# Sixteen small products of a blank tile ahead of TensorE's program

## The chip, the cores and the metric

The kernel runs on one core of a Trainium2 chip. A core has five engines that work side by side, each from its own list of instructions: TensorE (PE; its weight loads are listed apart, as PEld), VectorE (DVE), ScalarE (ACT), GpSimd (POOL) and SyncE (SP). They wait for each other and for transfers through semaphores. The metric is device time in microseconds. The kernel before takes 306.78 us, the median of three runs (306.5 to 307.46).

## The reference

Windowed attention with 8 batches of 8 heads over 576 positions, head size 64, and behind it a two-layer block on the 4608 tokens:

```python
scores = scale * np.matmul(q, k.transpose(0, 1, 3, 2))
rel = pos[:, None] - pos[None, :]
mask_plain = (rel >= 0) & (rel < window)                                  # window 32, heads 0-3
mask_dil = (rel >= 0) & (rel < window * dilation) & (rel % dilation == 0) # dilation 4, heads 4-7
scores = np.where(masks[None, :, :, :], scores, -1000000000.0)
attn = softmax(scores)                         # over the keys, 1e-9 added to the sum
x = matmul(attn, v)                            # then tokens by 512 features
h = x @ w_in                                   # 512 -> 2048
out = (h * (1.0 / (1.0 + np.exp(-h)))) @ w_out # 2048 -> 512
```

## The kernel before

Attention is cut into blocks of 32 queries by 64 keys. z = 0 names the four plain heads, z = 1 the four dilated ones, whose positions are sorted into four classes so that they become plain windows too. For each block TensorE makes the scores (L364, L374 and L390), DVE adds the mask, takes the maximum and normalises, ACT takes exponentials (L568; L557 for a whole tile), DVE turns the probabilities round (L606), and TensorE multiplies them with v (L637) into the transposed attention output, which copies put into xT (L670, L672, L707, L712). Layer one (L721, and L746 for batch 0) multiplies xT with w_in, ACT applies the SiLU into gT (L729, L754), layer two (L766, L790) multiplies gT with w_out, and the rows leave through SP (L776).

The order on each engine is the order of the program's text, since the scheduling is by hand: `plan_of(b)` says before which step of batch b's two layers which piece of attention for batches b+1 and b+2 is issued. Batch 0 has no layers to hide behind, so it has a prologue of its own (L896 to L935), and its attention is done in two parts of 256 and 320 positions, named `part`. The prologue runs: transposes of k and q for part 0 (L302 and L313, which read gT's space, where `load_part` has put the rows), scores (L390, L374), softmax, transposes for part 1, products with v, scores for part 1. Then comes layer one of batch 0: four feature tiles at a time for part 0 (products 256 columns wide), then two at a time for part 1 (320 wide). In `plan_of(0)`, `values0` and `finish0` for part 1 are placed at steps -8 and -6, that is among the layer-one products of part 0: their 64 and 44 products with v (L637) stand between 256-column products, and the two copies of L712 on DVE finish what the 320-column products read.

The loads are issued by POOL in the order of the text: k and q of batch 0 in two parts (L135), v of batch 0 (L174, L183), w_in in four pieces (L191), q and k of batch 1 (L112, L119), w_out in four pieces (L197), v of batch 1, and later batches from `plan_of`, q and k of them by L152.

Buffers come from pools. `cpool` (named const) holds single tiles for the whole run, among them the identity, the masks, both weights and gT; the pools opened after it (nat for loaded q and k, msp, stat, pp, ptp, xtp, o32) lie behind it in SBUF. Two pools are in PSUM: big, two buffers of two banks each, and ps, four buffers of one bank each, which transposes, scores and products with v use in turn.

TensorE's list holds 8799 instructions, nearly all of them pairs of a weight load and a product. The first of them are those of `transpose0(1, 1, 0, act)`, which wait for k's first part.

## Time and profile before

| | |
|---|---|
| median of three runs | 306.78 us (306.5 to 307.46) |
| the profiled execution | 307.47 us |
| its span, from first to last instruction | 305.7 us |
| TensorE products | busy 292.6 us, 96% of the span, 4393 of them |
| weight loads | busy 186.8 us, 4393 |
| DVE, ACT, POOL | busy 193.1, 203.8 and 120.0 us |
| software DMA queue q0 | 107840 packets, 20.38 MB |
| instruction queue q8 | 34 packets, 0.56 MB |
| mean granted TensorE clock | 0.998 |

A line of a list by time gives the start and the length in us, the engine, the line of the kernel, the operation with the tiles out<-in, the shapes and how many instructions are merged into the line; in square brackets stands the idle time of that engine just before, and what ended it. "issue" there means that the profile shows nothing that the engine waited for. The chain of waits is followed back from the last instruction: each piece is what the next one had to wait for.

### The profile page before, as it was taken

Reading aid. Unit: us, or ns where it says so; the run is one execution under the profiler, and the core shown is the slowest. Engines: PE = TensorE matmul, PEld = TensorE weight load, DVE = VectorE, ACT = ScalarE, POOL = GpSimd, SP = SyncE. Lnnn points to the kernel's source line nnn. Section 1 sums busy time; section 2 is a strip of 40 time slices with the busy share of each in tenths; the row PEclk is TensorE's granted clock in tenths of the full one; section 3 lists DMA queues with packets and bytes.
Section 4 is the critical chain, followed back from the end, with each engine's and each line's share of the span. In section 5 each row is a group of like instructions: output and inputs, shape, how many; then the busy total and the mean of one; then the engine's idle time right before and its main releaser. Section 6 shows DMA issues by size and latency. Waiting matters only on the chain.

```text
span 305.7 us, 10277 instructions
## 1 busy us (share of the span) xinstructions
PE 292.6 (96%) x4393; PEld 186.8 (61%) x4393; DVE 193.1 (63%) x353; ACT 203.8 (67%) x685; POOL 120.0 (39%) x182
## 2 busy tenths in 40 slices
PE   2998999999989999999999999999999999999995
PEld 1666754677445775477644775478644775477544
DVE  1895579448898868866893768955893762810012
ACT  3676597765997559975895559975795559546200
POOL 8745347979963295236906086240000000000000
PEclk9999999999999999999999999999999999999999
DMA  8999999999993899399959199390002100110021
GB/s 102 159 204 207 207 161 171 195 184 126 121 187 71 94 67 131 109 116 38 121 74 186 38 59 136 104 119 4 3 34 105 36 2 34 52 56 0 17 88 69
DMA packets 113213, 30.47 MB, mean 100 GB/s; under 512 B 95520, under 2 KB 108688, under 8 KB 113168
## 3 DMA queue, kind: packets, MB, share of 16 engines
q0 software_dynamic: 107840, 20.38, 80.8%
q1 hardware_dynamic: 5328, 9.44, 8.6%
q8 instruction: 34, 0.56, 0.8%
q14 instruction: 11, 0.09, 0.1%
HBM read 40.75 MB, written 9.44 MB: 164 GB/s over the span
## 4 chain that ended last, share of the span: by engine, by line
PE 78%; DMA 8%; DVE 5%; POOL 3%; ACT 3%; issue 2%; DVEq 0%; POOLq 0%
PE h L721 32%; PE o L790 31%; PE h L746 5%; PE x L637 4%; PE o L766 3%; DMA w_in<-in_moe_w_in_dram 3%; DMA n<-in_q_dram 2%; DMA gT<-in_q_dram 2%; ACT pe L568 2%; PE s L364 2%; POOL n L152 2%; DVE pn L590 1%; DMA vw<-in_v_dram 1%; POOL gT L135 1%; DVE ob L775 1%
## 5 line engine op out<-in xcount | busy, mean ns | idle before, releaser
L729 ACT ACTIVATE gT<-h 128x576 f16<-128x576 f32 x112 | 72.8, 650 | 61.5 <-PE h L721 61.3
L790 PE MATMUL o<-w_out,gT 128*128 128x512 f16 (+1 forms) x528 | 113.8, 373 | 0.0
L721 PE MATMUL h<-xT,w_in 128*128 128x288 f16 x896 | 113.4, 287 | 0.0
L721 PEld LDWEIGHTS <-w_in 128*128 128x128 f16 x896 | 86.5, 98 | 23.6 <-issue 0.2
L790 PEld LDWEIGHTS <-gT 128*128 128x128 f16 x528 | 50.6, 98 | 55.4
L568 ACT ACTIVATE pe<-ms,nm 128x64 f32<-128x64 f32 x238 | 78.9, 333 | 0.1
L775 DVE COPY ob<-o 128x512 f32<-128x512 f32 (+1 forms) x35 | 22.9, 664 | 51.8 <-PE o L790 50.6
L568 ACT ACTIVATION_READ_ACCUMULATOR pe<-ms,nm 128x1 f32 x238 | 44.5, 187 | 0.0
L152 POOL DMA_DIRECT2D n<-in_k_dram x44 | 31.9, 736 | 26.1 <-DVE kC L337 25.1
L408 DVE SCALAR_TENSOR_TENSOR ms<-s,mask 128x512 f32<-128x512 f32 x28 | 19.2, 686 | 29.1 <-PE s L364 19.9
L152 POOL DMA_DIRECT2D n<-in_q_dram x44 | 32.0, 744 | 2.5 <-DMA n<-in_q_dram 2.5
L174 POOL DMA_DIRECT2D vw<-in_v_dram x32 | 18.3, 578 | 35.3 <-PE x L637 33.0
L590 DVE TENSOR_TENSOR pn<-pe,r 128x640 f16<-128x640 f32 (+2 forms) x32 | 26.2, 818 | 1.1
L606 DVE STREAM_TRANSPOSE pt<-pn 128x640 f16<-128x640 f16 (+4 forms) x32 | 24.7, 772 | 1.1
L183 POOL DMA_DIRECT2D vw<-in_v_dram x32 | 21.2, 672 | 10.0 <-DMA w_out<-in_moe_w_out_dram 7.8
L488 DVE TENSOR_REDUCE nm<-ms 128x10 f32<-128x640 f32 (+1 forms) x28 | 22.0, 787 | 1.0
L746 PE MATMUL h<-xT,w_in 128*128 128x256 f16 (+1 forms) x128 | 19.2, 304 | 1.6 <-DVE band L244 0.9
L637 PEld LDWEIGHTS <-vw 32*64 32x64 f16 (+1 forms) x1264 | 13.0, 107 | 7.4 <-issue 7.1
L637 PE MATMUL x<-pt,vw 32*64 32x64 f16 (+2 forms) x1264 | 14.9, 193 | 1.7 <-DVE pt L606 1.7
L746 PEld LDWEIGHTS <-w_in 128*128 128x128 f16 x128 | 12.5, 104 | 6.3 <-issue 1.5
L766 PE MATMUL o<-w_out,gT 128*128 128x512 f16 x64 | 14.5, 380 | 0.0
L670 DVE CAST xT<-x 128x288 f16<-128x288 f32 x24 | 9.3, 449 | 7.7 <-PE x L637 7.7
(92 smaller groups left out, 204.6 us busy)
## 6 DMA issues: line engine op xcount, KB each, us to landing
out_dram<-ob SPq DMA_DIRECT2D x35, 256.0 KB, 3.4
n<-in_k_dram POOLq DMA_DIRECT2D x24, 108.0 KB, 4.2
n<-in_q_dram POOLq DMA_DIRECT2D x24, 108.0 KB, 4.9
vw<-in_v_dram POOLq DMA_DIRECT2D x31, 80.0 KB, 4.0
vw<-in_v_dram POOLq DMA_DIRECT2D x32, 72.0 KB, 3.9
w_in<-in_moe_w_in_dram POOLq DMA_DIRECT2D x4, 512.0 KB, 9.5
w_out<-in_moe_w_out_dram POOLq DMA_DIRECT2D x4, 512.0 KB, 11.4
n<-in_k_dram POOLq DMA_DIRECT2D x20, 72.0 KB, 4.0
```

The costliest lines, as they stand in the source:

```text
L152: nc.gpsimd.dma_start(out=qk[b, z, which][o : o + QB], in_=bass.AP((q, k)[which].tensor, (b * H + z * HH + half * HH // 2) * S * D + x * Q ...
L488: nc.vector.tensor_reduce(out=nm[:, 0:w], in_=ms[:, 0:w], axis=AX.X, op=ALU.max, negate=True)
L568: nc.scalar.activation(pe[:, t, :], src[t], AF.Exp, bias=a["nm", z, hi][:, t : t + 1], scale=k, accum_out=l[:, t : t + 1],)
L590: nc.vector.tensor_tensor(pn[:, 0:w], a["pe", z, hi][:, 0:w], r[:, 0:w, None].broadcast_to([P, w, KB]), ALU.mult)
L606: nc.vector.transpose(out, src)
L637: nc.tensor.matmul(x[h // 2][h % 2 * D : h % 2 * D + D, col : col + wd], vws[b % 2][r, NB + kb * DIL + c if z else kb], turned_cols(b, pt[ ...
L721: nc.tensor.matmul(h[:, half, 0:HS], w_in16[:, c, f * P : f * P + P], xT[c // 2][:, c % 2, half * HS : half * HS + HS], start=(c == cs[0]) ...
L729: nc.scalar.activation(gT[:, f, s0 : s0 + S].rearrange("p (a c) -> p a c", a=2), h[:, :, 0:HS], AF.Silu)
L746: nc.tensor.matmul(hs[i // m][:, i % m, 0 : c1 - c0], w_in16[:, c, (f + i) * P : (f + i + 1) * P], xT[c // 2][:, c % 2, c0:c1], start=(c = ...
L766: nc.tensor.matmul(o, gT[:, f, t * P : (t + 1) * P], w_out16[:, f, :], start=(f == 0), stop=(f == NFF - 1),)
L775: copy(ob, o)
L790: nc.tensor.matmul(o[:, 0, 0:m], gT[:, f, t * P : (t + 1) * P], w_out16[:, f, cols], start=(f == 0), stop=(f == NFF - 1),)
```

## The change

A tile `blank` of 32x32 half-precision zeros is added at the end of the constant pool, zeroed by DVE ahead of the memset of `band`. A tile `lead` is taken from ps, and sixteen products of `blank` with itself are written into its first 32 partitions and columns, ahead of the first transposes. Nothing reads `lead`. TensorE's list grows by 16 weight loads and 16 products to 8831 instructions, DVE's by one memset; the order of all other instructions on every engine is as it was. The first weight load of the sixteen waits for the memset on DVE, and the first product of the fourth transposed tile (L313 for q of part 0), which now gets the buffer that `lead` had, waits for the last of the sixteen.

```diff
     band = cpool.tile([P, KB], F32, name="band")
+    blank = cpool.tile([W, W], F16, name="blank")
+    nc.vector.memset(blank, 0.0)
     nc.vector.memset(band[0:W], 0.0)
     load_part(1, 0)
     load_part(0, 0)
...
+    lead = ps.tile([P, 512], F32, tag="ps", name="lead")
+    for _ in range(16):
+        nc.tensor.matmul(lead[0:W, 0:W], blank, blank, start=True, stop=True)
     transpose0(1, 1, 0, act)
     build_mask_b()
     transpose0(0, 1, 0, act)
```

## The prediction

> **What bounds the kernel now.** I read the page first, then the chain of waits, then TensorE's products and weight loads in order of time over the first 40 us, and at last the DMA queues and the busy time in chosen stretches.

> From the page: TensorE is the bound as a whole, and one DMA queue carries instructions.

> ```profile
> PE 292.6 (96%) x4393; PEld 186.8 (61%) x4393; DVE 193.1 (63%) x353; ACT 203.8 (67%) x685; POOL 120.0 (39%) x182
> PEclk9999999999999999999999999999999999999999
> q8 instruction: 34, 0.56, 0.8%
> ```

> The idle 4% lies mostly at the front, where the new work goes. The chain of waits between 12.9 and 33.5 us:

> ```profile
> 12.93 8.59 DMA w_in<-in_moe_w_in_dram
> 21.52 0.05 issue
> 21.56 1.92 PE h L746 x16
> ...
> 25.64 0.87 DVE xT L712 x2
> ...
> 27.13 0.47 issue
> 27.61 2.21 PE h L746 x15
> ...
> 33.52 0.01 issue
> 33.53 1.12 PE h L746 x7
> ```

> Until 21.5 us transfers decide; from 25.6 on TensorE does, with a gap before 27.6. In the lists by time, TensorE's products at the front and its weight loads around the gap:

> ```profile
> 5.64 0.60 PE L302 MATMUL t<-ident,gT 64*128 64x64 f16 x8 [5.64 <-DMA gT<-in_k_dram]
> ...
> 8.40 0.45 PE L390 MATMUL s<-kC,qC 64*32 64x64 f16 x32
> ...
> 17.88 3.48 PE L746 MATMUL h<-xT,w_in 128*128 128x256 f16 x16 [0.46 <-DMA w_in<-in_moe_w_in_dram]
> 21.56 1.92 PE L746 MATMUL h<-xT,w_in 128*128 128x256 f16 x16 [0.21 <-DMA w_in<-in_moe_w_in_dram]
> ```

> ```profile
> 25.03 0.43 PEld L637 LDWEIGHTS <-vw 32*64 32x64 f16 x44 [0.21 <-issue]
> 25.48 0.88 PEld L746 LDWEIGHTS <-w_in 128*128 128x128 f16 x9
> 27.60 1.88 PEld L746 LDWEIGHTS <-w_in 128*128 128x128 f16 x15 [1.24 <-issue]
> ```

> ```profile
> 27.59:33.52 5.93, 5.92 (x128) 4.05 (x128) 1.87 (x4) 3.88 (x7) 3.82 (x7) 1.00 1.22 206
> ```

> The reader is to see three things. (1) TensorE has no work before 5.64. (2) The idle 1.24 us before 27.60 has no tile behind it: "issue". The weight load that starts there waits for no semaphore; the last cast it could be tied to, the two of L712, ends at 26.51. (3) The last fence (busy time in a stretch: its columns are TensorE's products and weight loads, then DVE, ACT, POOL, the granted clock, DMA share and GB/s): from that stop to the next "issue" stop, at 33.53, TensorE ran 128 products and 128 weight loads, 256 instructions exactly.

> That number names the resource. 0.56 MB in 34 packets of q8 is 16.4 KB each, and 8799 TensorE instructions make some 34 portions of 256. Asked by stretches of 2 us, the DMA view has one q8 packet in each, and its row of GB/s jumps where it starts: 12.75, 19.15, 25.15, 31.20, 37.15, 43.25. At 3.0% of 16 engines over 2 us each lasts 0.96 us. So a portion is used 2.4 us after its fetch starts (25.17 to 27.60; 31.20 to 33.53), and the next fetch starts 3.6 us after the portion is begun (27.60 to 31.20, 33.53 to 37.17). In this stretch, with the DMA engines full of loads, TensorE can't get through 256 instructions in under 6.0 us, and twice it stops for them: from 26.51 (the end of the wanted cast) to 27.60, 1.09 us, and 0.18 us before 33.53.

> [...]

> **The change part by part.** The sum is made against the profiled execution: 307.47 us, span 305.70, 1.77 around it. It stands 0.69 above the median of 306.78, so I add the sum to the median.

> *The memset.* Nearest rows: 85 ns for 32 columns, 112 for 64 (L230, L204); their starts stand 0.07 to 0.12 apart. It goes ahead of the zeroing of band, which POOL needs at 3.27, 2.3 us later, and DVE then idles 1.77 us to 3.35. Zero. Uncovered: 0.1. It might stretch POOL's first DMA issue, which ran beside such memsets for 0.81 against 0.69 for the next: 0 to 0.07; I take 0.

> *The sixteen products.* None of this size is in the trace. Cheapest row: 32 products of 64x32 weights in 0.45 us, 14 ns each; dearest: the eight of L302 in 0.60 us, 75 each. So 0.2 to 1.2 us, nearer the first as the weights are small. They can start when the memset ends, about 1.0, and end by 2.2; TensorE then still waits for in_k until 5.64. Zero; uncovered, 0.2 to 1.2.

> *Buffers and addresses.* lead takes one of the four ps buffers, so the fourth transpose tile (L313 for q, at 7.82) waits for the last of the sixteen, done 5 us before; no other wait changes, and the later tiles keep their order. The pools after const move up 64 bytes. No row prices that: k and q loads of one shape land in 4.2 and 4.9 us, so an address is worth less than 0.7 on one landing, either way, and none of those landings is what the chain waits for at 40 us. Zero.

> *The 32 instructions themselves.* This is the step with a price. They run in idle time, but every 256-instruction portion now begins 32 instructions earlier in the old code. Two effects.

> First, the chain of fetches starts earlier. The portion start whose crossing let the fetch of 12.75 go lies among the L374 scores at 9.3; moved by 32 it lies among the L390 scores at 8.40. TensorE's queue takes instructions ahead of running them (at 49.3 a fetch starts 0.5 us after its crossing is executed, not 3.6), which puts the old crossing near 8.5 and the new near 8.2: 0.3 earlier. Bounds: 0, if transfers ahead of it fix the fetch's start, and 0.9, if nothing is taken ahead. I take 0.3, by the row at 49.3.

> Second, the stop moves. The portion usable at 27.60 is now usable at 27.30, but it begins 16 pairs earlier: 9 of L746 and the last 7 of the 44 L637 products. In the trace those 7 start at 25.31, and from there to where the 27.60 work could have begun is 1.26 us (7 products, their two casts on DVE to 26.51, 0.06 for the semaphore; 9 of L746 at 0.109 beside them). Before, these 1.26 us ran ahead of the stop, hidden by the fetch; now they come behind it: 27.30 + 1.26 = 28.56 against 27.60, +0.96. The next portion is there at 33.2, and TensorE reaches its start at 32.96 + 0.96 = 33.9: the 0.18 stop goes, +0.78. The one after (39.2) is reached at 40.2, unhindered; no stop is seen there now either.

> Behind that TensorE waits twice, 0.37 at 72.6 and 1.31 at 89.3, both for DVE work that began on TensorE's own products (at 66.97 and 79.99), so these move along. What runs beside what on DVE and POOL at 86.7, where a multiplication of 0.83 us takes 1.65, may shift and give or take 0.3. Sum: **+0.78 us, 306.78 + 0.78 = 307.6**; with the bounds of the first effect (1.08 with no earlier start, 0.18 with 0.9) and that 0.3, -0.1 to +1.4.

> **The rivals.**

> *Fetches don't decide, or it is swallowed.* For it: most of the 34 portions show no stop, and the gap at 27.6 ends near the SiLU of L754 (26.57 to 27.59), so that could be the cause; against it, the products there use the other big buffer, and 256 between two stops. 306.8.

> *A stop vanishes (the other side).* If the portion now beginning in the L637 products is there by 25.3, no stop is left: -1.09 - 0.18, 305.5. It decides from a fetch that starts before 23.0, 2.2 us sooner than now. Against: the first crossing gains 0.9 at most; for: lags of 0.5 (49.3) exist when the DMA engines are less loaded.

> *More starvation.* If the moved starts meet short products (the 36 transposes at 39.4, the 64 scores at 66.5) when a fetch is late, another stop of about 1 us adds up: 308.5. It decides where a fetch starts less than 2.4 us before need; the nearest, at 64.5 for 66.94, has just that.

> *The clock.* The sixteen products of L746 at 17.88 stand 0.213 apart, those at 21.56 0.109: the array runs at half rate until about 21, though the granted clock is 1.00. If the new work raised it early, those at 17.88 would end at 19.6 and wait for w_in until 21.5 all the same: 306.8. [...]

> **How the numbers follow.** The shifted stop: 0.62. Nothing, by either reason: 0.15. A stop vanishes: 0.11. More starvation: 0.12. What a measurement of this kernel can tell from no change is about 0.3%, 0.92 us: the shifted stop's +0.78, with its bounds, lies beyond that in 0.25 of the 0.62. So slower 0.25 + 0.12 = 0.37, same 0.37 + 0.15 = 0.52, faster 0.11. The range leaves out the vanished stop and the upper part of the starvation: 306.3 to 308.5; the likeliest case's own is 306.7 to 308.2.

> **What would show it.** Sixteen products at about 1 us, and the first L302 still at 5.64. A weight load of L637, 7 from the end of its 44, after an idle 1.5 to 2 us marked "issue" and starting near 27.3; nothing of the kind before the first 128x320 products, which start near 28.6; 128 and 128 from stop to stop, if there is a second; the q8 jumps 0.3 us sooner. The prediction is wrong if the stop sits where it sat, if the L637 products run through, or if TensorE is 0.8 late at 40 us and not at the end.

## The result and the profile after

| | before | changed |
|---|---|---|
| median of 12 runs, us | 306.86 (306.08 to 307.96) | 309.25 (306.97 to 310.98) |
| ratio, 95% interval | | 1.0058, 1.0034 to 1.0082 |
| profiled execution, us (span) | 307.47 (305.7) | 310.91 (309.1) |
| its mean granted clock | 0.998 | 0.994 |

The change makes the kernel slower, by more than 0.3%. The median lies 0.75 us above the top of the forecast range (308.5) and 1.65 us above the forecast (307.6). The changed kernel also scatters more: 4.0 us from lowest to highest, against 1.9. Four of its twelve executions have a mean clock of 0.994 and are the four of 310.08, 310.42, 310.91 and 310.98 us (the profiled one is among them); the other eight have 0.999 or more and a median of 308.2. Ratios here and below are not quotients of the two medians, and leave out executions 1.5% or more above the fastest of their kernel (one and two of the 35 of the kernel before in the later sets).

The page of the changed kernel: 16 products and 16 weight loads more, no other count that matters, and one slice in which the clock was not fully granted.

```profile
PE 295.6 (96%) x4409; PEld 188.6 (61%) x4409; DVE 194.0 (63%) x354; ACT 203.8 (66%) x685; POOL 119.5 (39%) x182
PEclk9999999999998999999999999999999999999999
q8 instruction: 34, 0.56, 0.8%
```

TensorE's products of the changed kernel by time (start, length of the group, line, tiles, shape, count; in brackets the idle time ahead and what ended it). Line numbers are 2 higher than in the kernel before, so L639 is the old L637, L748 the old L746; from the new products on they are 5 higher.

```profile
0.93 0.61 PE L900 MATMUL lead<-blank 32*32 32x32 f16 x16 [0.93 <-DVE blank L205]
5.66 0.60 PE L304 MATMUL t<-ident,gT 64*128 64x64 f16 x8 [4.13 <-DMA gT<-in_k_dram]
...
26.11 0.50 PE L639 MATMUL x<-pt,vw 32*64 32x32 f16 x37
27.58 0.24 PE L639 MATMUL x<-pt,vw 32*64 32x64 f16 x7 [0.98 <-issue]
27.75 3.40 PE L748 MATMUL h<-xT,w_in 128*128 128x256 f16 x24
...
89.08 0.41 PE L639 MATMUL x<-pt,vw 32*64 32x64 f16 x28
91.20 0.66 PE L639 MATMUL x<-pt,vw 32*64 32x64 f16 x48 [1.71 <-DVE pt L608]
91.79 6.91 PE L792 MATMUL o<-w_out,gT 128*128 128x512 f16 x24
```

Three places matter. The sixteen products run in 0.61 us, in the dead time ahead of the first transpose, which still starts at 5.66. At 27.58 stands the moved stop, 37 into the group of 44, as foretold. And at 91.20 a wait has grown, with something new behind it: the 24 products of L792 take 6.91 us, where the kernel before has

```profile
87.60 0.41 PE L637 MATMUL x<-pt,vw 32*64 32x64 f16 x28
89.32 0.61 PE L637 MATMUL x<-pt,vw 32*64 32x64 f16 x48 [1.31 <-DVE pt L606]
89.86 5.36 PE L790 MATMUL o<-w_out,gT 128*128 128x512 f16 x24
```

Setting each TensorE instruction of the changed trace against the same one before gives where the time went. The delay is +0.75 us at 7.3, as a load landed later in that execution, and +1.08 at 25.3, ahead of the stop: the trace's clock record begins, at full rate, at 23.30 us there and at 21.10 in the kernel before, and up to then the first products of layer one stand 0.21 apart, not 0.11. The stop takes this delay up, since it ends 2.46 us after its fetch starts (27.58 against 25.12), as in the kernel before (27.60 against 25.18, 2.42), and not with TensorE's work. Behind it the delay is +1.17 at 33.5, then +1.48 at 72.6 (0.3 came near 56), +1.88 behind the wait at 91.2, and then 0.21 more with every product of L792 until it is +3.49 at 95; from there it stays (+3.35 at the end). So the loss is 1.2 at the stop, 0.3 near 56, 0.4 in the longer wait, 1.6 behind it.

The weight loads of the changed kernel around the stop, in the same columns, have the row that the prediction asked for; 37 pairs of the 44 end one portion, and the other 7 begin the next.

```profile
26.11 0.39 PEld L639 LDWEIGHTS <-vw 32*64 32x64 f16 x37 [0.21 <-issue]
27.58 0.14 PEld L639 LDWEIGHTS <-vw 32*64 32x64 f16 x7 [1.09 <-issue]
```

Now the wait. VectorE of the changed kernel up to the pt (the probabilities turned round) that ends it:

```profile
87.65 1.50 DVE L589 TENSOR_SCALAR r<-l 128x10 f32<-128x10 f32 x1
89.19 0.22 DVE L590 RECIPROCAL r<-r 128x10 f32<-128x10 f32 x1
89.44 0.82 DVE L592 TENSOR_TENSOR pn<-pe,r 128x640 f16<-128x640 f32 x1
90.30 0.84 DVE L608 STREAM_TRANSPOSE pt<-pn 128x640 f16<-128x640 f16 x1
```

and GpSimd of the same kernel at that time: its transfers' issues, then a subtraction of the maximum for batch 3 (the old L543).

```profile
85.43 2.62 POOL L152 DMA_DIRECT2D n<-in_q_dram  x4
88.06 1.05 POOL L545 TENSOR_TENSOR ms<-ms,nm 128x512 f32<-128x512 f32 x1
```

The TENSOR_SCALAR on ten columns, 0.13 to 0.17 us where it runs alone, takes 1.50 and ends 0.04 after GpSimd's operation. It began 0.41 ahead of that operation, under the last of the four transfer issues (87.39 to 88.05), and by its own length would have been through under that issue. So it was held through the rest of an issue and then the whole operation. In the kernel before it was the TENSOR_TENSOR of 0.83 that took 1.65:

```profile
86.74 1.65 DVE L590 TENSOR_TENSOR pn<-pe,r 128x640 f16<-128x640 f32 x1
```

```profile
85.11 2.65 POOL L152 DMA_DIRECT2D n<-in_q_dram  x4
87.74 1.54 POOL L543 TENSOR_TENSOR ms<-ms,nm 128x512 f32<-128x512 f32 x1
```

It too began under an issue and by its own length would have ended at 87.57, ahead of GpSimd's operation, which itself took 1.54 there, against 1.05 in the changed kernel. Here VectorE's row ends 0.89 us ahead of GpSimd's (88.39 against 89.28), not 0.04 behind it, and both are lengthened. What the two engines hold each other up over is in no trace.

That GpSimd's issues of transfers hold VectorE by themselves is seen where its operation has been taken out (a run described below):

```profile
86.58 0.39 DVE L591 TENSOR_SCALAR r<-l 128x10 f32<-128x10 f32 x1
```

This row ends with an issue of GpSimd (86.31 to 86.97). In the fourteen traces of this document 27 TENSOR_SCALARs of this line behind 30 us, 0.31 to 0.56 us long, end within 0.01 us of the end of an issue. It hangs on the moment: all 27 that begin 0.25 to 0.35 us into an issue are held (over 0.30 us long), and three of the 102 that begin at another point of one. The 0.3 us near 56 are of this kind: a TENSOR_SCALAR from 54.95 to 55.46, 0.51 long (0.17 in the kernel before), ends with an issue, and the products behind its pt come that much later.

Last, busy time in two neighbouring stretches of 3.41 us (TensorE's products, weight loads, DVE, ACT, POOL, then granted clock, DMA share, GB/s), of the changed kernel

```profile
87.98:91.39 3.41, 1.70 (x58) 0.83 (x59) 3.31 (x5) 3.41 (x22) 1.12 (x2) 1.00 1.88 192
91.40:94.80 3.40, 3.40 (x55) 1.43 (x42) 3.30 (x9) 3.40 (x20) 0.00 (x0) 0.53 0.51 126
```

and of the kernel before

```profile
87.98:91.39 3.41, 2.10 (x60) 1.22 (x56) 3.36 (x8) 3.41 (x21) 1.30 (x1) 1.00 1.65 227
91.40:94.80 3.40, 3.40 (x17) 1.54 (x16) 3.22 (x7) 3.40 (x20) 0.00 (x0) 1.00 0.16 43
```

After a stretch with TensorE busy for 1.70 us the clock was granted at half for the next stretch (0.53 on the mean of the row); after one with 2.10 it was not (1.00). The products of L792 stand 0.43 apart instead of 0.21 while it lasts. In each trace's clock record the clock changes only at whole multiples of 3.41 us from the first entry (in the changed kernel half rate from 91.57 to 94.98, twenty of them behind 23.30), so these stretches have fixed borders, and a wait may fall into one or across two. Counted by these borders over all fourteen traces, half rate followed the four stretches up to 300 us in which TensorE was busy for 1.59 to 1.86 us, and none with 2.11 (the kernel before, 85.96 to 89.37) or more; in the last 10 us of the kernel three with 1.50 to 1.89 were not followed by it, so the busy time is not the whole condition.

### The profile page after: what moved, and what is told of

Same layout as the page of the kernel before. It is cut to its first block, busy times and chain, and to the rows that moved or that the text cites. A ratio compares the mean times of both kernels' runs of the same rounds, so it can differ in the third digit from the quotient of the medians.

```text
span 309.1 us, 10310 instructions
## 1 busy us (share of the span) xinstructions
PE 295.6 (96%) x4409; PEld 188.6 (61%) x4409; DVE 194.0 (63%) x354; ACT 203.8 (66%) x685; POOL 119.5 (39%) x182
## 4 chain that ended last, share of the span: by engine, by line
PE 68%; DMA 17%; POOL 5%; DVE 4%; ACT 3%; issue 2%; POOLq 0%
PE h L723 32%; PE o L792 31%; DMA w_out<-in_moe_w_out_dram 4%; DMA n<-in_k_dram 4%; DMA w_in<-in_moe_w_in_dram 4%; PE x L639 3%; DMA gT<-in_q_dram 2%; ACT pe L570 2%; PE s L366 2%; POOL n L152 2%; DMA vw<-in_v_dram 1%; DVE pn L592 1%; POOL w_in L191 1%; DVE r L589 1%; POOL gT L135 1%
## 5 line engine op out<-in xcount | busy, mean ns | idle before, releaser
L792 PE MATMUL o<-w_out,gT 128*128 128x512 f16 (+1 forms) x528 | 115.3, 376 | 0.0
L792 PEld LDWEIGHTS <-gT 128*128 128x128 f16 x528 | 51.1, 99 | 56.5 <-issue 2.1
L592 DVE TENSOR_TENSOR pn<-pe,r 128x640 f16<-128x640 f32 (+2 forms) x32 | 25.3, 792 | 1.1
L748 PE MATMUL h<-xT,w_in 128*128 128x256 f16 (+1 forms) x128 | 19.5, 311 | 0.4 <-DVE ms L479 0.4
L639 PEld LDWEIGHTS <-vw 32*64 32x64 f16 (+1 forms) x1264 | 13.2, 107 | 9.1 <-issue 8.1
L639 PE MATMUL x<-pt,vw 32*64 32x64 f16 (+2 forms) x1264 | 15.2, 193 | 3.2 <-DVE pt L608 2.1
L748 PEld LDWEIGHTS <-w_in 128*128 128x128 f16 x128 | 12.9, 106 | 4.9 <-DMA w_in<-in_moe_w_in_dram 0.6
```

Of the source, the lines that this page charges most:

```text
L592: nc.vector.tensor_tensor(pn[:, 0:w], a["pe", z, hi][:, 0:w], r[:, 0:w, None].broadcast_to([P, w, KB]), ALU.mult)
L639: nc.tensor.matmul(x[h // 2][h % 2 * D : h % 2 * D + D, col : col + wd], vws[b % 2][r, NB + kb * DIL + c if z else kb], turned_cols(b, pt[ ...
L748: nc.tensor.matmul(hs[i // m][:, i % m, 0 : c1 - c0], w_in16[:, c, (f + i) * P : (f + i + 1) * P], xT[c // 2][:, c % 2, c0:c1], start=(c = ...
L792: nc.tensor.matmul(o[:, 0, 0:m], gT[:, f, t * P : (t + 1) * P], w_out16[:, f, cols], start=(f == 0), stop=(f == NFF - 1),)
```

## The experiments

The theory after the result: the sixteen products cost nothing themselves; their 32 instructions move the stop, which makes TensorE late; the lateness brings VectorE's work into GpSimd's operation near 88, and the longer wait lets the clock fall. Rivals: the added work itself, the buffer it takes, or the memset; a fault of the stop alone; the half clock being chance. Every ratio is against runs of the kernel before on the same chip.

### How many products: 1, 8, 104, 128

```diff
-    for _ in range(16):
+    for _ in range(1):     # and 8, 104, 128
         nc.tensor.matmul(lead[0:W, 0:W], blank, blank, start=True, stop=True)
```

One product, which keeps memset, tile and buffer and leaves out 30 of the 32 instructions:

> One product instead of sixteen: the blank tile, its memset, the buffer taken from ps and the 64 bytes stay, but TensorE's list is longer by 2 instructions, not 32. Theory (the fetched portions of 256 begin elsewhere): the portion that is usable at 27.6 us begins with the last weight load of the gap itself, so the stop stays where the kernel before has it, and the time is that of the kernel before, 306.9, within 0.5 us. Rival (memset, buffers, addresses or the first product as such): as slow as the changed kernel, 309.2.

Eight:

> Eight products, 16 instructions. Theory of the portions: the stop falls before the last 8 of the 256-column products of layer one, ends at 27.6 as ever, and 8 x 0.109 us of work that stood ahead of it now stands behind: TensorE is 0.85 us late at 28.5 us and 0.7 at 40, against 1.25 and 1.15 for sixteen; time between the kernel before and the changed one, 307.6. Rival (work of the products): half of the changed kernel's loss, 308.0; rival (memset, buffers, addresses): 309.2.

A hundred and four:

> 104 products, 208 instructions, which end by 5 us, ahead of the first transposes. Theory of the portions: they begin 48 instructions later in the old code than in the kernel before; the stop at 27.6 finds TensorE at work until 28.7, so it is gone (-1.09), that at 33.5 too (-0.18), and the portion usable at 39.5 begins behind the eight 320-column products that end at 39.7: 305.6; if the first fetch starts up to 0.85 us later because its crossing stands behind the wait for q's second part, 306.5. Faster than the kernel before in either case. Rival (work, or anything that grows with the number of products): slower than the changed kernel.

A hundred and twenty-eight, one whole portion:

> 128 products, 256 instructions, one whole portion: every portion begins at the same old instruction as in the kernel before. Theory: the stop of 1.1 us is back before 27.6, none among the products with v, and the time is that of the kernel before, 306.9, within 0.5 us. Rival (work of the products): eight times the work, slower than the changed kernel. Rival (the leading work moves the array's clock): half-rate products of layer one at 17.9 us gone, time different from both.

| products | median, us (lowest to highest) | ratio (95%) | span of the profiled run, us |
|---|---|---|---|
| before | 306.79 (306.04 to 308.11) | | |
| 1 | 307.19 (306.06 to 308.69) | 1.0019 (0.9998 to 1.0040) | 304.3 |
| 8 | 307.06 (306.51 to 310.81) | 1.0026 (0.9993 to 1.0058) | 308.0 |
| 104 (four runs) | 308.40 (307.96 to 308.45) | 1.0045 (1.0028 to 1.0063) | 306.6 |
| 128 | 307.07 (306.33 to 308.54) | 1.0008 (0.9988 to 1.0027) | 304.8 |

The place of the stop follows the count. With one product the weight loads show it where it was, behind 8 loads of layer one (9 before):

```profile
25.00 0.77 PEld L748 LDWEIGHTS <-w_in 128*128 128x128 f16 x8
27.29 1.74 PEld L748 LDWEIGHTS <-w_in 128*128 128x128 f16 x14 [1.52 <-DVE band L246]
```

The bracket names a copy on VectorE because the load behind this stop waits on a semaphore of VectorE; but that copy was through by 26.8, half a microsecond before. In thirteen of the fourteen traces TensorE's weight loads have a stop of 0.8 us or more between 24 and 40 us; these stops end 2.30 to 2.51 us after a fetch starts, this one 2.38.

With eight it has moved by 8 pairs and leaves one in front (16 move it by 16, into the 44):

```profile
25.07 0.10 PEld L748 LDWEIGHTS <-w_in 128*128 128x128 f16 x1
27.00 1.83 PEld L748 LDWEIGHTS <-w_in 128*128 128x128 f16 x16 [1.84 <-issue]
```

With 128, 256 instructions, it is back behind nine:

```profile
25.79 0.88 PEld L748 LDWEIGHTS <-w_in 128*128 128x128 f16 x9
27.65 1.34 PEld L748 LDWEIGHTS <-w_in 128*128 128x128 f16 x11 [0.98 <-issue]
```

That settles the portion of 256. The 128 products, which keep the memset and the buffer and do eight times the work, cost at most 0.27% by their interval, where the changed kernel costs at least 0.34%; so none of the three is the cause. Eight products are a half case: their median is that of one product, below the 307.6 expected, and TensorE was 0.3 late at 40 us in the trace, not 0.7, as the fetch near 25 us came 0.58 sooner. But two of the ten executions were at half rate for a time, the profiled one among them: 309.90 us, with the wait (1.55 us ahead of 90.14) and half rate behind it, as in the changed kernel.

A hundred and four were a miss. They were to move both stops out of the way and make the kernel faster; the two stops did go (the 128x320 products that the kernel before begins at 27.60 come at 26.63, 0.97 sooner), but a later one took their place. Weight loads of that kernel:

```profile
33.90 0.14 PEld L392 LDWEIGHTS <-qC 64*32 64x32 f16 x17 [0.26 <-issue]
35.53 0.14 PEld L392 LDWEIGHTS <-qC 64*32 64x32 f16 x15 [1.49 <-issue]
```

The fetches there start at 6.34, 12.93, 19.23, 26.72 and 33.18, against 12.76, 19.19, 25.18, 31.20 and 37.18 before: where the loop of loads needed a fetch about every 6 us, one came 7.5 us after the last. An attempt to keep the fetch's place with four products more gave

> 108 products, 216 instructions: portions begin 40 instructions later in the old code than in the kernel before, so that the stop of 27.6 falls behind eight products of layer one that the kernel before runs after it; with 104 the chain of fetches lost a place (a portion begun at 23.7, fetched at 26.7, usable at 29.1 and the next at 35.5). Theory: if the portion that begins in the products with v near 23 us is reached before its fetch is due, the chain keeps its places (27.6, 33.6, 39.6) and TensorE is 0.7 us early at 42 us: 306.1. If it loses a place as with 104: a stop of 1.5 us near 35, 308.4.

and 307.84 us (306.83 to 309.42; ratio 1.0026, 1.0002 to 1.0050), with the fetches again at 19.52, 27.11 and 33.61 and a stop of 1.2 us among the same scores: less dear, not a gain. No count tried beats the kernel before.

### Taking GpSimd's operation away

Batch 3's first plain tile goes without the subtraction of its maximum; the quotient of the softmax stays the same. First in the kernel before, then in the changed one:

```diff
-            at(21, shift, 3, 0, 0, nc.gpsimd)
+            at(21, unshifted, 3, 0, 0)      # only notes the tile as shifted
```

> The kernel before without GpSimd's one tensor operation (the 512-column addition of the negated maximum for one tile of batch 3, 1.05 us and more near 87 us); the exponential of that tile takes the scores as they are, which for a softmax gives the same quotient. Nothing is added in front. Theory (VectorE's operations next to it are held until GpSimd's ends, and TensorE waits for them): the wait of 1.31 us before 89.3 falls under 0.4, the executions above 307.2 go, median 306.2. Rival (that wait has another cause): 306.8 and the wait as before.

> The changed kernel, sixteen products, with the same GpSimd operation taken out. Theory (two parts: the fetch stop moved to 7 products from the end of the 44 costs 1.2 to 1.5 us in every execution; the rest of the loss comes from the meeting of VectorE and GpSimd near 88 us, which TensorE's lateness makes certain, and from the half-rate stretch that follows the longer wait in some executions): no wait over 0.5 us near 90, no execution with a clock under 0.998, median 1.2 to 1.5 us above the same kernel without the products, 307.5, and all executions within 1 us. Rival (the spread and the loss come from the fetch stop alone): 309.2, from 307 to 311.

The changed kernel itself ran beside them on the same chip:

> The changed kernel itself, beside the others on the same chip. Theory: the stop ends at 27.6 with 7 products of the 44 behind it, in this execution too; TensorE 1.1 to 1.5 us late at 60 us against the kernel before; a wait between 0.2 and 1.8 us near 90 us according to where VectorE meets GpSimd; half rate from 91 to 95 only if that wait is above 1.3 us. Median 309, executions from 307 to 311.

| | median, us (lowest to highest) | ratio (95%) | span of the profiled run, us |
|---|---|---|---|
| before | 306.76 (305.74 to 310.33) | | |
| before, without the operation | 306.85 (306.04 to 308.22) | 0.9995 (0.9975 to 1.0016) | 304.0 |
| changed, without the operation | 307.25 (306.51 to 309.03) | 1.0012 (0.9985 to 1.0039) | 305.2 |
| changed | 308.92 (307.65 to 310.49) | 1.0062 (1.0035 to 1.0089) | 308.2 |

In the changed kernel without the operation the stop is where it was, and the wait is gone; TensorE's products, L643 being the old L637:

```profile
26.84 0.24 PE L643 MATMUL x<-pt,vw 32*64 32x64 f16 x7 [1.27 <-issue]
...
88.26 1.14 PE L643 MATMUL x<-pt,vw 32*64 32x64 f16 x76
```

Beside it the changed kernel, whose same 28 products come at the same time:

```profile
88.28 0.41 PE L639 MATMUL x<-pt,vw 32*64 32x64 f16 x28
90.24 0.61 PE L639 MATMUL x<-pt,vw 32*64 32x64 f16 x48 [1.55 <-DVE pt L608]
```

So of the loss of 2.16 us on this chip 1.67 go with one GpSimd operation, while the median of the kernel before loses nothing to it: the 306.2 expected there was a miss. Its wait of 1.31 is thus no fixed feature of the kernel before, as I had read it, but one of that profiled execution and its like. Some executions do pay: 7 of the 35 beside these runs and 8 of the 35 beside the next took 308.3 us or more, none of the 24 without the operation. Taking it away also frees ScalarE's exponentials of that tile from waiting for GpSimd, which was not tested apart; but the VectorE rows ahead of the wait are back at 0.15 and 0.83 us in the trace of the changed kernel without it.

What is left there, 0.40, goes with the moved stop. Three of those twelve executions (308.32, 308.35 and 309.03 us) have a mean clock of 0.994, where none was expected, and the twelve spread over 2.5 us, not 1. The trace of the changed kernel itself has the stop and the wait as expected, but TensorE is only 0.68 late at 60 us. Both kernels without the operation were run a second time:

> The kernel before without GpSimd's tensor operation, a second time, for the pair with and without products: 306.8; TensorE at the first 320-column product 2.4 us after the fetch that starts near 25 us.

> The changed kernel without GpSimd's tensor operation, a second time. Theory: 3.7 us from that fetch to the first 320-column product, and the median 0.8 to 1.4 us above the same kernel without the products, where the first pair gave 0.4 by medians and 1.2 by traces. Rival (the moved stop is swallowed later): 0.4 or less again.

They gave 307.41 (306.94 to 308.25; ratio 1.0003, 0.9981 to 1.0026) and 307.36 (306.72 to 310.40; ratio 1.0016, 0.9987 to 1.0045). Taking both runs together, 24 executions each: medians 307.25 without and 307.33 with the sixteen products, a difference of 0.09 us (95% interval -0.2 to 0.74); means 307.20 and 307.69, a difference of 0.48 (0.07 to 0.94). Seven of the 24 with the products took 308.3 us or more, none of the 24 without. Six of these seven have a mean clock of 0.994, which none of the 24 without has. The other 18 have a mean 0.05 us above the 24 without (95% interval -0.25 to 0.34). So the stop alone costs about half a microsecond on average, and nearly all of it in the executions with a stretch at half rate, for which GpSimd's operation is not needed; where in them that lies is in no trace. In the others the lateness of TensorE is not seen at the end. In the second pair of traces it shrinks from 0.57 to 0.16 us near 89, where the kernel without the products waits 0.53 for VectorE; in the first pair it stays at 1.2. Where it goes in the rest is not shown.

### Late without the products

The kernel before, with nothing at the front, and nine idle products of 320 columns at 27 us, whose output is overwritten, to make TensorE late by about as much:

```diff
+        for _ in range(9 if (f, part) == (0, 1) else 0):
+            nc.tensor.matmul(
+                hs[0][:, 0, 0 : c1 - c0], w_in16[:, 0, 0:P], xT[0][:, 0, c0:c1], start=True, stop=True
+            )
```

> The kernel before, with nothing at its front, but nine idle products of 320 columns (0.137 us each) ahead of the first 320-column products of layer one, which start at 27.6; their results are written over. TensorE is then late by about 1.2 us at 29 us, as in the changed kernel, with the portions of instructions where they were up to there. Theory (the loss comes from being 1.2 us late at 28 us, by whatever cause, and grows near 90 us where VectorE meets GpSimd): 308.6, executions up to 310.5 among them, wait before 90 us of 1 us or more. Rival (the products at the front do something of their own): 306.8 + 1.0 = 307.8, no wait that is longer than the kernel before shows.

It took 308.83 us (307.4 to 310.81; ratio 1.0051, 1.0022 to 1.0079), near the changed kernel's 308.92, but 1.60 above the 307.23 of the kernel before beside it; the interval, 0.7 to 2.4 us, holds the rival's 1.0 as well. So the traces have to tell the two apart. TensorE is 1.58 us late at 40 us in this one, where the changed kernel had 1.16, as the fetch near 25 us came half a microsecond later too. The operation of 0.83 us takes 2.15 there and the wait is 1.63, as a row of VectorE and one of TensorE show:

```profile
88.17 2.15 DVE L590 TENSOR_TENSOR pn<-pe,r 128x640 f16<-128x640 f32 x1
```

```profile
91.25 0.61 PE L637 MATMUL x<-pt,vw 32*64 32x64 f16 x48 [1.63 <-DVE pt L606]
```

That is the longer wait of the theory. Nothing at the front was needed for it in this trace: a TensorE that is late from 28 us on was enough. The profiled execution has no half rate (clock 1.0, span 307.6): its wait lies across the border of two stretches at 90.30, busy for 2.73 and 2.46 us. Three of the twelve executions have a mean clock of 0.994.

### Keeping TensorE busy in the wait

The changed kernel with twelve idle products of 288 columns put into the wait at 90, to keep the clock; their output is overwritten.

```diff
+        for _ in range(12 if (b, z) == (2, 0) else 0):
+            nc.tensor.matmul(
+                xs[0][0][:, 0:HS], ident, gT[:, 0, 0:HS], start=True, stop=True, skip_group_check=True
+            )
```

> The changed kernel with twelve idle products of 288 columns (1.4 us) put ahead of batch 2's first products with v, where TensorE later waits 1.5 to 1.7 us; their results are written over. Theory (half rate from 91 to 95 us follows from TensorE's idleness in the 3.4 us before): no execution with a clock under 0.998, the products after the wait stand 0.21 apart instead of 0.43; the executions above 309.3 go, median 308.2. Rival (the clock falls for another reason): half rate in a third or more of the executions as in the changed kernel, median 309 or more.

The median was 308.99 us (307.77 to 311.17; ratio 1.0057, 1.0029 to 1.0085), which missed the expected 308.2, and five of the twelve executions, the profiled one among them, have a clock of 0.994 or less after all. The place that was filled has no half rate, the 24 products of layer two taking 5.35 us again; but GpSimd's operation was over there before VectorE came to it (87.24 to 88.33 against 88.53), so that this execution shows little of what the filling does. The half rate stands behind the moved stop instead. Products of TensorE there, and busy time in two stretches around it:

```profile
26.82 0.24 PE L639 MATMUL x<-pt,vw 32*64 32x64 f16 x7 [1.82 <-issue]
26.99 4.88 PE L752 MATMUL h<-xT,w_in 128*128 128x256 f16 x24
```

```profile
23.60:27.00 3.40, 1.58 (x53) 1.11 (x51) 0.87 (x2) 2.26 (x4) 1.35 (x3) 1.00 1.19 209
27.02:30.40 3.38, 3.38 (x22) 2.19 (x16) 2.34 (x7) 1.02 (x1) 2.70 (x5) 0.50 1.21 209
```

TensorE was busy for 1.58 us of the stretch ahead, near the 1.70 of the changed kernel at 88. That the half rate comes of the idleness ahead of it is supported by this, not shown to be its only condition. The two places were not told apart for executions without a trace, so how many have it at 27 and how many at 91 stays open, and so does what keeps the median at 309.

## Why the prediction was wrong where it was, point by point

**The memset, the sixteen products, buffers and addresses: right.** Products at 0.93 to 1.54, the first transpose at 5.66 (5.64 before). One product and 128 cost the same, and the late kernel without any of them loses as much as the changed one.

**"The 32 instructions themselves", the stop: right in mechanism, place and size.** It stands 7 products from the end of the 44, begins its weight load at 27.58 after 1.09 us marked "issue" (foretold near 27.3 after 1.5 to 2), and the stop before 33.53 is gone. The 128x320 products that the kernel before begins at 27.60 (its second; the first stood ahead of the stop) come at 28.81, foretold near 28.6. From the fetch's start near 25 us to those products it takes 3.61 to 3.69 us in the four traces with sixteen products and no idle ones (4.50 in the fifth, at half rate behind the stop), 3.32 with eight, and 2.30 to 2.53 in the five without products or with one or 128: +1.2, against the +1.26 of the working.

**"The chain of fetches starts earlier", 0.3: right on the average of the traces, not in the profiled execution.** There the fetch near 25 starts 0.05 us sooner (25.12 against 25.18). Over the traces it starts at 25.08 on the mean of five without the shift (24.60 to 25.37) and at 24.73 on that of four with sixteen products (24.40 to 25.12): 0.35 sooner, though the two groups overlap, so that this is little more than agreement. That TensorE's queue takes instructions ahead of running them was my estimate from one lag, of 0.5 us (a portion begun at 48.75, a fetch at 49.28) against 3.6; no run tested it apart. The two together give about +0.85 at 29 us, where the prediction had +0.96, or +0.78 behind the second stop. That much was right. That it moves along to the end was not: with GpSimd's operation taken out it reaches the end as 0.48 on the mean (0.07 to 0.94), and as 0.05 without the executions at half rate.

**The step that failed: "What runs beside what on DVE and POOL at 86.7 … may shift and give or take 0.3", with the waits that "move along".** The wait of 1.31 was taken as one of VectorE's work that began on TensorE's own products, and so would move with it. But much of it was GpSimd's doing (0.82 us of lengthening, by its issues of transfers or its operation), and GpSimd does not move with TensorE: its operation comes when its issues of transfers are through, at 87.22, 87.74 and 89.35 in the traces of 1, no and 128 products and at 87.10, 87.24, 88.06 and 88.57 in four of a late TensorE, while VectorE's operations ahead of that pt move with it. With one product and with 128 their TENSOR_TENSOR was done before GpSimd's operation began, and the waits were 0 and 0.16 us. The question to ask was not how long the meeting is but how often it happens, and how late VectorE would have to be for it to happen always. The page's trace showed the meeting in one execution, and I took it for the rule. In the runs the median of the kernel before loses nothing by it (306.76 with, 306.85 without the operation), and that of the changed kernel 1.67 us (308.92, 307.25), where the prediction had allowed 0.3.

**A term that the sum lacked: the half clock behind a long wait.** The rival on the clock looked at the front alone. The wait of 1.71, with 1.70 us of work in a stretch of 3.41, was followed by a stretch at half rate and +1.6 us. Four of twelve executions of the changed kernel have the mean clock of 0.994 that goes with one such stretch, five of twelve when it was run again, and two and three of 35 of the kernel before beside it. Gaps of 1.71 us (the changed kernel, ahead of 91.20) and 1.82 us (with the idle products, ahead of 26.82), with some idling around them, preceded half rate here.

**The rivals.** The clock at the front was read from the spacing of the products, and rightly; the granted clock of 1.00 ahead of 21 us was not a reading, as the trace's clock record only begins at 21.10. That fetches don't decide fell with the four counts. More starvation, a further late fetch, had the right side but the wrong resource: no further stop is seen in the changed kernel; it is what 104 products ran into. A vanished stop came true with 104 products and was paid for by that same late fetch. The likeliest case ended at 308.2 because its upper bound held only the fetch's 0 to 0.9 and the 0.3, and the range at 308.5, the price of one more stop; the executions of the changed kernel reached 310.98.

**Open.** Where VectorE was held for longer than GpSimd's operation lasts (the changed kernel twice, eight products, the late kernel), its row had begun 0.4 to 0.5 us ahead of it, under the last issue. Why a row that begins at one moment of an issue is held and one at another is not, no run shows. Nor is it shown why three stretches with little work near the end were not followed by half rate, and where the lateness goes in executions that have neither the long wait nor half rate.

## What to carry to other kernels

Where loads fill the DMA engines (206 GB/s from 27.59 to 33.52 us here), count a changed kernel's instructions ahead of its first stops as well as its work: 32 cost 2.39 us (309.25 against 306.86), while their sixteen products ran in 0.61 us of idle time, and 256 cost nothing that ten runs could tell (307.07 against 306.79). When an engine gets later, look for the work of another engine that keeps its own time, and ask where the two will meet, since a wait shown in one trace may be one that most executions miss. Sum the idleness in stretches of the clock record (3.41 us here) too: the wait of 1.71 us, half of one, cost 1.6 us more behind it.
